# Part-ahead joins, closer search steps and alternating transpose banks in a retention plus two-layer expert kernel

## The chip, the cores and the metric

One core of a Trainium2 chip runs the whole program. The metric is the device time of one execution in microseconds (us); lower is better. Where a profile is shown, it is of one execution recorded by the hardware profiler.

## The reference, cut to what matters

Three blocks run one after the other on 3072 tokens of 512 features.

```python
# 1. retention (attention without softmax), 4 x 8 heads, 768 steps, 64 wide
state = gamma * state + k_t (outer) v_t ;  y_t = q_t @ state / 8
# 2. a dense layer: w_in 512 x 2048, w_out 2048 x 512
x2 = (s * relu(x @ w_in) ** 2 + b) @ w_out
# 3. eight experts, 512 -> 1024 -> 512, cap = 3072 / 8 = 384 tokens each
logits = x2 @ w_gate
for idx in argsort(-logits.flatten()):          # the highest (token, expert) pair first
    tok, e = idx // 8, idx % 8
    if assigned[tok] >= 0 or counts[e] >= cap: continue
    assigned[tok] = e; counts[e] += 1
for e in range(8):
    out[assigned == e] = relu(x2[assigned == e] @ w1[e]) @ w2[e]
```

The greedy assignment is done as up to eight searches: each finds by counting the threshold at which the next expert fills up, so the experts are known one after the other.

## The kernel before, in words

Every product of two float32 matrices is three matmuls on parts: a "high" part (`h`, `hh`, `gh`, `rh`), rounded by ScalarE, and a "low" part (`l`, `hl`, `gl`, `rl`), the rest, made by VectorE. The change touches the last 460 us: the end of block 2 and all of block 3.

- **The last dense blocks** (`x_last`, L672): 64 units of three 128x512 matmuls each; their four results are scaled by ScalarE (L675) and written to DRAM as `x2d` (L677).
- **A search** (`search`, with `begin` ahead of it). `begin` takes each token's best remaining expert, makes the one-hot `Eh`, and ScalarE copies it out as `EH` (L767), the stationary operand of the counts. Then come six steps; a step is a compare on VectorE (`cmp`, L772: 128x1512 against 63 thresholds in the first two, 128x744 against 31 in the other four), 24 small matmuls that count (L779), and a short VectorE chain (`sat`, `tr`, `jj`, `thr`) that ends in the next compare. A last count (`g`, 128x2), a sum over tokens (L865, `tots` L867) and two matmuls (L880, L881) give each token its place in the expert.
- **An index** (`index`): four one-hot comparisons (`big`, L915), 24 matmuls (L921), and `idx`, the token numbers of this expert. **A fetch** (`fetch`): three indirect DMAs of 128 rows of `x2d` each into `big` (GpSimd's queue, L935), 12 transposes (L945), `gh` and `gl`.
- **An expert** (`mlp`): for each of eight parts `f`, four `eh_unit`s (three 128x384 matmuls each, L997) make the hidden part, ScalarE makes `hh` (L1000), VectorE `hl` (L1006), and three `ey_unit`s (three 128x512 matmuls each, L1018) add it to the output. Weights come as `eraw` (512 KB a part, SyncE's queue, L966); `prep` splits them into `h` (ScalarE, L974) and `l` (VectorE, L975).

The order is set while the program is written out: `Weave` adds up planned costs of units on TensorE (490 for an `eh_unit`, 650 for an `ey_unit` or an `x_last` unit), and each side generator (searches, indexes, weights, fetches) goes on when that sum passes its due time. The numbers in the generators' `yield`s are therefore distances in planned TensorE nanoseconds. `Weave.until` lets the sides run on without units until an expert's `gh`, `gl` exist. Each engine executes its own instructions in the order written. PSUM has eight banks; the searches count into bank 6, the index uses 7, the experts' hidden parts 2 and 3, their outputs 0, 1 and 4, and the transposes 5 (for the first expert 4 and 5).

Of the kernel before, what the change touches and what calls it, by code (L numbers as in the profile page):

```python
# [20 lines left out]
F32 = mybir.dt.float32  # L21
F32R = mybir.dt.float32r
# [5 lines left out]
AF = mybir.ActivationFunctionType  # L28
OP = mybir.AluOpType
# [52 lines left out]
def kernel(  # L82
# [17 lines left out]
    PRO=1.5,  # L100
    PN=2,
    CY=(700, 1200, 650),
    SY=(5500, 5200, 4200, 3000, 2600, 1200),
    IY=(1500, 2700, 900),
    LG=(900, 880),
    FE=(7110, 3450),
    FZ=(8390, 160),
    BG=(800,),
    WARM=24,
):  # L110
    nc = tc.nc
# [6 lines left out]
    KC = Dm // 128  # L118
    NF = w64.shape[0]
    E, NF2 = w12.shape[0], w12.shape[1]  # L120
    CAP = N // E
    GT = CAP // 128
    NC = N // 128
# [12 lines left out]
    PE, ACT, DVE, POOL, SP = nc.tensor, nc.scalar, nc.vector, nc.gpsimd, nc.sync  # L136

    def bank(i):
        return psum.tile([128, 512], F32, name=f"b{i}", tag=f"b{i}")
# [69 lines left out]
    wb = bank(3)[:, 0:TB]  # L209
# [363 lines left out]
    while not a3.done:  # L573
        if conv.due < a3.due and PN not in READY:
            t = conv.due
# [5 lines left out]
    wv = Weave([conv])  # L581
# [16 lines left out]
    for blk in range(3, NB - 2):  # L598
        nxt = Side(attn(blk + 1, False) if blk < NB - 3 else attn2())
        wv.add(nxt)  # L600
        units = moe1((blk,), ((0, 1),), 2)
# [12 lines left out]
    ident = rt.tile([128, 128], F32, name="ident")  # L614
# [9 lines left out]
    ones_b = rt.tile([128, 128], BF, name="ones_b")  # L624
# [101 lines left out]
    def b3(ap, n):  # L726
        return ap[:, :, None].to_broadcast([128, NC, n])

    def b8(ap):
        return ap[:, None, :].to_broadcast([128, NC, E])  # L730
# [12 lines left out]
    def begin(i):  # L743


        Lm = rt.tile([128, NC, E], F32, name="Lm")
        if i:
            DVE.tensor_tensor(Lm, L, b8(pen), op=OP.add)
            src = Lm
        else:  # L750
            src = L
        m = rt.tile([128, NC], F32, name="m", bufs=2)
        mx = rt.tile([128, NC], F32, name="mx", bufs=2)
        DVE.tensor_reduce(m, src, axis=AX.X, op=OP.max)
        if i:
            yield BG[0]
        DVE.tensor_tensor(Lm, src, b3(m, E), op=OP.is_equal)
        DVE.tensor_tensor(Lm, Lm, b8(w8), op=OP.mult)
        DVE.tensor_reduce(mx, Lm, axis=AX.X, op=OP.max)
        if i:  # L760
            yield BG[0]
            DVE.tensor_tensor(mx, mx, Uf, op=OP.mult)
        Eh = rt.tile([128, NC, E], BF, name="Eh")
        DVE.tensor_tensor(Eh, b8(w8), b3(mx, E), op=OP.is_equal)

        EH = rt.tile([128, NC, 128 // E, E], BF, name="EH")
        ACT.activation(EH, Eh[:, :, None, :].to_broadcast([128, NC, 128 // E, E]), AF.Copy)  # L767
        ME[i] = (m, mx, EH.rearrange("p c r e -> p c (r e)"))

    def compare(m, thr, n):  # L770
# [5 lines left out]
    def count(EH, x, n):  # L776
        ps = bank(6)
        for c in range(NC):
            PE.matmul(ps[:, 0:n], EH[:, c, :], x[:, c, 0:n], start=(c == 0), stop=(c == NC - 1))  # L779
        return ps  # L780
# [10 lines left out]
    def search(i):  # L791
        last = i == E - 1
        m, mx, EH = ME.pop(i)
        if last:
            T = rt.tile([128, 1], F32, name="T")
            DVE.memset(T, NEG)
            yield SY[0]
        else:
# [3 lines left out]
            for s, w in enumerate(BW):  # L802
                n = (1 << w) - 1
                sh -= w
                yield SY[0] if s == 0 else SY[1] if n == NT else SY[2]
                cnt = count(EH, cmp, n)
# [39 lines left out]
        DVE.tensor_tensor(eq, eq, ug, op=OP.subtract)  # L846
        yield SY[3]

# [12 lines left out]
        DVE.tensor_tensor(rem, rem, ca[:, 0:1], op=OP.subtract)  # L861
        yield SY[4]

# [11 lines left out]
        DVE.tensor_tensor(rem, rem, s8, op=OP.add)  # L875
        yield SY[5]
        while i - 2 in SLOT or i - 2 >= 0 and i - 2 not in EREG:
# [13 lines left out]
    def index(i):  # L891

        while i not in SLOT:
            yield 200
        yield IY[0]
        s1 = SLOT.pop(i)
# [17 lines left out]
        for c in range(0, NC, 6):  # L914
            DVE.tensor_tensor(ob[:, c:c + 6, :], iota16[:, None, :].to_broadcast([128, 6, 128]),  # L915
                              lowp[:, c:c + 6, None].to_broadcast([128, 6, 128]), op=OP.is_equal)
            yield IY[2]
        for c in range(0, NC, 6):
            yield IY[2] if c else IY[1] - IY[2]
            for c in range(c, c + 6):  # L920
# [8 lines left out]
    def fetch(i):  # L929

        while i not in IDX or not X2DONE:
            yield 200
        xg = rt.tile([128, GT, Dm], F32, name="big", bufs=1)
        for t in range(GT):
            POOL.indirect_dma_start(out=xg[:, t, :], out_offset=None, in_=x2d[:, :],  # L935
                                    in_offset=bass.IndirectOffsetOnAxis(ap=IDX[i][:, t:t + 1], axis=0))
        yield FE[0] if i else FZ[0]
        while i - 2 >= 0 and i - 2 not in DONE or (i, 1) not in EW_ASKED:
            yield 200
        gh = ff.tile([128, KC, CAP], F32R, name="gh")  # L940
        gl = ff.tile([128, KC, CAP], F32R, name="gl")
        for kc in range(KC):
            pt = bank(5 if i or kc % 2 else 4)
            for t in range(GT):
                PE.transpose(pt[:, t * 128:(t + 1) * 128], xg[:, t, kc * 128:(kc + 1) * 128], ident)  # L945
            ACT.activation(gh[:, kc, :], pt[:, 0:CAP], AF.Identity, bias=cT[:, kc:kc + 1])
            DVE.scalar_tensor_tensor(gl[:, kc, :], pt[:, 0:CAP], cT[:, kc:kc + 1], gh[:, kc, :].bitcast(F32),  # L947
                                     op0=OP.add, op1=OP.subtract)
            if kc < 2:
                prep(i, kc)  # L950
            if kc < KC - 1:
                yield FE[1] if i else FZ[1]
        XG[i] = (gh, gl)

    DONE = set()
# [2 lines left out]
    EREG = {}  # L958

    EW_ASKED = set()  # L960

    def e_load(i, f):
        EW_ASKED.add((i, f))
        t = stage.tile([128, 2, 512], F32, name="eraw", tag="sa" if f % 2 else "sb")
        ERAW[i, f] = t
        SP.dma_start(t, w12[bass.ds(EREG[i], 1), f].rearrange("o p a n -> p (o a) n"))  # L966

    def e_split(i, f):
        raw = ERAW.pop((i, f))
        for a in range(2):  # L970
            n = 16 * (i % 2) + 2 * f + a
            hi = wpool.tile([128, 512], F32R, name=f"h{n}", tag=f"h{n}")
            lo = wpool.tile([128, 512], F32R, name=f"l{n}", tag=f"l{n}")
            ACT.activation(hi, raw[:, a, :], AF.Copy)  # L974
            DVE.tensor_tensor(lo, raw[:, a, :], hi.bitcast(F32), op=OP.subtract)  # L975
            EW[i, f, a] = (hi, lo)

    def prep(i, f):
        if f < NF2 and (i, f, 0) not in EW:
            e_split(i, f)  # L980
            if f + 4 < NF2:
                e_load(i, f + 4)
# [6 lines left out]
    def eh_unit(i, f, part):  # L989
        gh, gl = XG[i]  # L990
        wh, wl = EW[i, f, 0]
        if part == 0:
            PH[0] = bank(2 + f % 2)[:, 0:CAP]
        kc = part
        ks = slice(kc * 128, (kc + 1) * 128)
        for n, (a, b) in enumerate(((wh, gh), (wh, gl), (wl, gh))):
            PE.matmul(PH[0], a[:, ks], b[:, kc, :], start=(kc == 0 and n == 0), stop=(kc == KC - 1 and n == 2))  # L997
        if part == KC - 1:
            hh = ff.tile([128, CAP], F32R, name="hh")
            ACT.activation(hh, PH[0], AF.Relu)  # L1000
            HH[i, f] = [hh, PH[0]]

    def eh_out(i, f):
        hh, ph = HH[i, f]
        hl = ff.tile([128, CAP], F32R, name="hl")
        DVE.scalar_tensor_tensor(hl, ph, 0.0, hh.bitcast(F32), op0=OP.max, op1=OP.subtract)  # L1006
        HH[i, f] = (hh, hl)

# [21 lines left out]
    def mlp(i):  # L1030
        units = []

        for f in range(NF2 + 1):
            if f < NF2:
                for part in range(KC):
                    units.append((490, lambda f=f, part=part: eh_unit(i, f, part)))
            for t in range(GT):

                for g in (f - 1,) if f < NF2 - 1 else () if f < NF2 else (f - 2, f - 1):
                    if g >= 0:  # L1040
                        units.append((650, lambda g=g, t=t: ey_unit(i, g, t)))
                if f < NF2 and t == 0:
                    units.append((0, lambda f=f: (eh_out(i, f), prep(i, f + 2))))
                if f == NF2:
                    units.append((0, lambda t=t: e_out(i, t)))
        return units

    def searches():
        for i in range(E):
            yield from search(i)  # L1050
# [15 lines left out]
    def fetches():  # L1066
        for i in range(E):
            yield from fetch(i)

    list(begin(0))  # L1070
    wv = Weave([Side(searches()), Side(indexes()), Side(weights())])
    fill(len(order))
    X2DONE.append(1)
    p1.close()
    ff = ctx.enter_context(tc.tile_pool(name="ff", bufs=2))
    wv.add(Side(fetches()))
    for i in range(E):
        wv.until(lambda: i in XG)
        for u in mlp(i):
            wv.unit(*u)  # L1080
        DONE.add(i)
# [81 lines left out]
```

## Time and profile before

| | us |
|---|---|
| median of three runs | 1107.38 (1106.67 to 1112.36) |
| the profiled execution | 1106.38 |
| its span, first to last instruction | 1104.3 |
| TensorE busy / weight loads busy | 1006.6 (91%) / 877.4 (79%) |
| VectorE / ScalarE / GpSimd busy | 769.6 (70%) / 460.6 (42%) / 78.0 (7%) |

The times of the rows below are of the profiled execution, whose span leaves 2.1 us of its time outside. Busy times of matmuls overlap their successors, so a busy TensorE may still advance slowly. Mean TensorE clock over the span was 0.962 of full.

### The profile page before, as it was taken

The page shows a single profiled execution, that of the slowest core. Times are in us where ns is not written, and L with a number is a line of the kernel's source. Part 1 is how long each engine was busy: PE and PEld are TensorE (multiplying, and loading weights), DVE is VectorE, ACT ScalarE, POOL GpSimd, SP SyncE. Part 2 cuts the span into 40 slices and gives each one's busy share as a digit, 9 for nine tenths or more (in the row PEclk, how much of TensorE's full clock was granted, in tenths as well). Part 3 has the DMA queues.
Part 4 walks back from the last instruction along what each step waited for, and adds up shares of the span by engine and source line. Part 5 has one row for each costly group of instructions (what it writes and reads, how often), then busy time and mean ns, then how long its engine had stood idle before and what let it go on. Part 6 is the DMA issues. An engine that isn't in the chain of part 4 may idle for free.

```text
span 1104.3 us, 19566 instructions
## 1 busy us (share of the span) xinstructions
PE 1006.6 (91%) x7636; PEld 877.4 (79%) x7636; DVE 769.6 (70%) x1954; ACT 460.6 (42%) x978; POOL 78.0 (7%) x99
## 2 busy tenths in 40 slices
PE   5699999899999999999999998596888898888997
PEld 4698878889899989889988986484767777676786
DVE  2899992587887878787726243777868787876642
ACT  1367665344444444444436621233323333343442
POOL 3200010000000000000000000102020201111211
PEclk8899999899999999999999999598899999999999
DMA  8343433432121212121211002223242434333540
GB/s 305 109 143 115 153 135 124 135 105 56 60 68 48 68 49 77 50 66 49 68 39 33 1 1 99 84 96 97 76 133 98 134 97 144 114 106 106 173 142 29
DMA packets 35036, 104.48 MB, mean 95 GB/s; under 512 B 4736, under 2 KB 5248, under 8 KB 34944
## 3 DMA queue, kind: packets, MB, share of 16 engines
q1 hardware_dynamic: 30528, 89.60, 24.7%
q0 software_dynamic: 3840, 12.59, 3.4%
q8 instruction: 60, 0.98, 0.4%
q10 hardware_dynamic: 576, 1.05, 0.3%
q14 instruction: 32, 0.26, 0.1%
HBM read 90.64 MB, written 12.58 MB: 93 GB/s over the span
## 4 chain that ended last, share of the span: by engine, by line
PE 66%; DVE 15%; issue 8%; DMA 6%; ACT 3%; POOL 2%; SPq 0%; POOLq 0%; DVEq 0%; ACTq 0%
PE b L415 22%; PE b L444 18%; PE b L997 6%; PE b L1018 5%; PE b L672 3%; DMA big<-x2d,idx 3%; PE b L779 2%; DVE l L975 2%; PE b L348 2%; PE b L358 2%; PE b L328 2%; DVE cmp L772 2%; POOL big L935 2%; DVE raw L268 1%; DVE raw L253 1%
## 5 line engine op out<-in xcount | busy, mean ns | idle before, releaser
L467 DVE SCALAR_TENSOR_TENSOR scr<-tmp,wg 128x512 bf16<-128x512 f32 x288 | 198.0, 688 | 8.8 <-ACT tmp L454 4.0
L415 PE MATMUL b<-xh,h 128*128 128x256 f32 x704 | 200.0, 284 | 1.4 <-DVE xls L367 1.4
L415 PE MATMUL b<-xh,l 128*128 128x256 f32 x704 | 199.6, 284 | 0.0
L415 PE MATMUL b<-xl,h 128*128 128x256 f32 x704 | 199.6, 284 | 0.0
L418 ACT ACTIVATE r<-b 128x256 f32<-128x256 f32 x192 | 73.3, 382 | 208.0 <-PE b L415 199.9
L415 PEld LDWEIGHTS b<-xh,h 128*128 128x128 f32 x704 | 135.0, 192 | 10.2 <-DVE xls L367 1.6
L415 PEld LDWEIGHTS b<-xl,h 128*128 128x128 f32 x704 | 135.0, 192 | 5.5
L415 PEld LDWEIGHTS b<-xh,l 128*128 128x128 f32 x704 | 135.0, 192 | 0.0
L444 PE MATMUL b<-h,rl 128*128 128x512 f32 x320 | 126.0, 394 | 3.5 <-DVE rl L434 3.5
L444 PE MATMUL b<-h,rh 128*128 128x512 f32 x320 | 128.9, 403 | 0.0
L444 PE MATMUL b<-l,rh 128*128 128x512 f32 x320 | 126.0, 394 | 0.0
L434 DVE TENSOR_TENSOR rl<-r,rh 128x256 fp32r<-128x256 f32 x160 | 68.7, 430 | 46.7 <-ACT rh L427 46.2
L1018 PE MATMUL b<-h,hh 128*128 128x512 f32 x192 | 81.1, 423 | 13.3 <-ACT hh L1000 13.3
L997 PE MATMUL b<-gh,h 128*128 128x384 f32 x256 | 93.3, 364 | 0.0
L997 PE MATMUL b<-gl,h 128*128 128x384 f32 x256 | 88.0, 344 | 1.6 <-DVE gl L947 1.6
L1000 ACT ACTIVATE hh<-b 128x384 fp32r<-128x384 f32 x64 | 31.3, 489 | 137.8 <-PE b L997 136.3
L975 DVE TENSOR_TENSOR l<-eraw,h 128x512 fp32r<-128x512 f32 x128 | 82.3, 684 | 7.6 <-ACT h L974 7.6
L997 PE MATMUL b<-gh,l 128*128 128x384 f32 x256 | 87.5, 342 | 0.0
L1018 PE MATMUL b<-h,hl 128*128 128x512 f32 x192 | 79.0, 411 | 5.1 <-DVE hl L1006 4.6
L426 ACT ACTIVATE r<-r 128x256 f32<-128x256 f32 x192 | 79.9, 416 | 5.1
L1018 PE MATMUL b<-l,hh 128*128 128x512 f32 x192 | 77.3, 403 | 0.0
L444 PEld LDWEIGHTS b<-h,rl 128*128 128x128 f32 x320 | 60.1, 188 | 20.5 <-DVE rl L434 7.2
(191 smaller groups left out, 1816.9 us busy)
## 6 DMA issues: line engine op xcount, KB each, us to landing
eraw<-in_w_dram SPq DMA_DIRECT2D x64, 512.0 KB, 3.5
q<-in_qkv_dram SPq DMA_DIRECT2D x36, 512.0 KB, 4.8
raw<-in_w_dram SPq DMA_DIRECT2D x32, 512.0 KB, 4.3
first<-in_qkv_dram SPq DMA_DIRECT2D x24, 256.0 KB, 6.5
qdec<-in_dec_dram SPq DMA_DIRECT2D x24, 256.0 KB, 2.8
x2d<-tmp SPq DMA_DIRECT2D x20, 256.0 KB, 3.5
wg<-in_wgT_dram SPq DMA_DIRECT2D x4, 512.0 KB, 6.7
x2d<-tmp ACTq DMA_DIRECT2D x4, 256.0 KB, 2.0
```

The source lines that it names most:

```text
L328: PE.matmul(ps[s][:, p * 128:(p + 1) * 128], kT[ss, p, :], qT[ss, p, :], start=(p == 0), stop=True, skip_group_check=True)
L415: PE.matmul(ph, a[:, ks], b[:, kc, :], start=(n == 0), stop=(n == 3 * KC - 1))
L418: ACT.activation(r, ph, AF.Relu)
L426: ACT.activation(r, r, AF.Square)
L434: DVE.tensor_tensor(rl, r, rh.bitcast(F32), op=OP.subtract)
L444: PE.matmul(X2[blk][t], a[:, ts], b, start=(f == 0 and i == 0), stop=(f == NF - 1 and i == 2))
L467: DVE.scalar_tensor_tensor(scr, x, 1.0, WG[e], op0=OP.mult, op1=OP.mult, accum_out=of[:, e:e + 1])
L672: PE.matmul(XB[c], a[:, cs], b, start=(f == 0 and i == 0), stop=(f == NF - 1 and i == 2))
L975: DVE.tensor_tensor(lo, raw[:, a, :], hi.bitcast(F32), op=OP.subtract)
L997: PE.matmul(PH[0], a[:, ks], b[:, kc, :], start=(kc == 0 and n == 0), stop=(kc == KC - 1 and n == 2))
L1000: ACT.activation(hh, PH[0], AF.Relu)
L1018: PE.matmul(Y[i, t], a[:, ts], b, start=(f == 0 and j == 0), stop=(f == NF2 - 1 and j == 2))
```

## The change

- Numbers: the distances between a search's steps (`SY`), inside `begin` (`BG`) and inside an index (`IY`) get smaller; a fetch's distance from its DMAs to its first transpose (`FE[0]`) grows and that between its transposes (`FE[1]`) shrinks.
- `EH` is copied in four quarters instead of one instruction.
- Transposes alternate between banks 5 and 7; the first expert's use banks 4, 5, 0 and 1, and go by fetched tile instead of by feature block.
- An expert's outputs (`ey_unit`) follow its hidden parts by two instead of one, `prep` runs three parts ahead instead of two, and the low part of a weight is made at the next `prep`, not at once. `hh` and `hl` get a third buffer.
- After the last dense unit, 28 matmuls on constants (128x512, into bank 3, not read) stand in TensorE's order.

```diff
-    SY=(5500, 5200, 4200, 3000, 2600, 1200),
-    IY=(1500, 2700, 900),
+    SY=(3200, 3800, 3200, 2500, 2200, 800),
+    IY=(600, 1800, 800),
-    FE=(7110, 3450),
-    FZ=(8390, 160),
-    BG=(800,),
+    FE=(9000, 3000),
+    FZ=(8390, 1300),
+    BG=(450,),
...
-        ACT.activation(EH, Eh[:, :, None, :].to_broadcast([128, NC, 128 // E, E]), AF.Copy)
+        for c in range(0, NC, 6):
+            ACT.activation(EH[:, c:c + 6], Eh[:, c:c + 6, None, :].to_broadcast([128, 6, 128 // E, E]), AF.Copy)
+            if i:
+                yield BG[0]
...
-        while i - 2 >= 0 and i - 2 not in DONE or (i, 1) not in EW_ASKED:
+        while i - 2 >= 0 and i - 2 not in DONE or (i, 2) not in EW_ASKED:
...
+        if i == 0:
+            for f in range(3):
+                prep(i, f)
+            pts = [bank(b) for b in (4, 5, 0, 1)]
+            for t in range(GT):
+                for kc in range(KC):
+                    turn(pts[kc], t, kc)
+                if t < GT - 1:
+                    yield FZ[1]
+            prep(i, NF2)
...
-            pt = bank(5 if i or kc % 2 else 4)
+            if i:
+                pt = bank((5, 7)[kc % 2])
...
-            DVE.tensor_tensor(lo, raw[:, a, :], hi.bitcast(F32), op=OP.subtract)
+            ELOW.append((lo, raw[:, a, :], hi))
...
     def prep(i, f):
+        while ELOW:
+            lo, raw, hi = ELOW.pop(0)
+            DVE.tensor_tensor(lo, raw, hi.bitcast(F32), op=OP.subtract)
...
-                for g in (f - 1,) if f < NF2 - 1 else () if f < NF2 else (f - 2, f - 1):
+                for g in (f - 2,) if f < NF2 else (f - 2, f - 1):
...
-                    units.append((0, lambda f=f: (eh_out(i, f), prep(i, f + 2))))
+                    units.append((0, lambda f=f: (eh_out(i, f), prep(i, f + 3))))
...
+    wb = bank(3)
+    for _ in range(28):
+        wv.unit(220, lambda: PE.matmul(wb, ones_b, ones_b[:, None, :].to_broadcast([128, 4, 128]), start=True, stop=True))
```

What this does to the order is shown at three places. The first is VectorE, at the end of the first search. Before:

```order
L861 TENSOR_TENSOR rem<-rem,b_7542 128x1
L975 TENSOR_TENSOR l_7608<-eraw,h_7607 128x512
L975 TENSOR_TENSOR l_7612<-eraw,h_7611 128x512
L867 CAST tots<-b_7620 128x128
L869 TENSOR_TENSOR Uf<-Uf,ug 128x24
```

With the change:

```order
L864 TENSOR_TENSOR rem<-rem,b_7506 128x1
L870 CAST tots<-b_7576 128x128
...
L918 TENSOR_TENSOR big<-iota_6403,lowp 128x768
L762 TENSOR_TENSOR mx<-mx,Uf 128x24
L764 TENSOR_TENSOR Eh<-c_6397,mx 128x192
L918 TENSOR_TENSOR big<-iota_6403,lowp 128x768
L1004 TENSOR_TENSOR l_7569<-eraw,h_7568 128x512
L1004 TENSOR_TENSOR l_7572<-eraw,h_7571 128x512
```

The low parts of the first weights have moved from ahead of `tots` to behind the first two one-hot comparisons of the index.

The second place is ScalarE in the second or third expert, where the next search begins. Before:

```order
L1000 ACTIVATE hh<-b_9535 128x384
L974 ACTIVATE h_9566<-eraw 128x512
L974 ACTIVATE h_9570<-eraw 128x512
L767 ACTIVATE EH<-Eh 128x3072
L1000 ACTIVATE hh<-b_9595 128x384
```

With the change:

```order
L1026 ACTIVATE hh<-b_8801 128x384
L996 ACTIVATE h_8840<-eraw 128x512
L996 ACTIVATE h_8843<-eraw 128x512
L768 ACTIVATE EH<-Eh 128x768 x2
L1026 ACTIVATE hh<-b_8848 128x384
L768 ACTIVATE EH<-Eh 128x768
L996 ACTIVATE h_8906<-eraw 128x512
L996 ACTIVATE h_8909<-eraw 128x512
L768 ACTIVATE EH<-Eh 128x768
L1026 ACTIVATE hh<-b_8912 128x384
```

The one long copy, which stood between two `hh`, has become quarters with `hh` and weight splits between them.

The third place is TensorE at the end of the first expert (before) and, with the change, where the transposes for the second expert end. Before (of each count's 24 pairs the first is shown):

```order
L945 MATMUL b_8624<-ident,big 128x128 x3
L779 LDWEIGHTS EH
L779 MATMUL b_8630<-cmp,EH 128x31
...
L945 MATMUL b_8668<-ident,big 128x128 x3
L997 MATMUL b_8674<-gh,h_8518 128x384
L997 MATMUL b_8674<-gl,h_8518 128x384
L997 MATMUL b_8674<-gh,l_8519 128x384
```

With the change:

```order
L1044 MATMUL b_8233<-h_8387,hh 128x512
L1044 MATMUL b_8233<-l_8388,hh 128x512
L1044 MATMUL b_8233<-h_8387,hl 128x512
L947 MATMUL b_8745<-ident,big 128x128 x3
L1044 MATMUL b_8242<-h_8281,hh 128x512
L1044 MATMUL b_8242<-l_8282,hh 128x512
L1044 MATMUL b_8242<-h_8281,hl 128x512
L782 LDWEIGHTS EH
L782 MATMUL b_8758<-g_8721,EH 128x2
```

Before, the last transposes and counts stood between two experts with no expert unit among them; now the last transposes stand among the units of the expert that ends.

## Rows read from the trace of the kernel before

**Rows 1.** Windows: the join, then the eight experts; its first line names the columns

```profile
core 0: us, PE busy (x) PEld busy (x) DVE busy (x) ACT busy (x) POOL busy (x), PEclk, DMA share, GB/s
684.80:716.50 31.70, 12.86 (x122) 9.97 (x122) 21.09 (x62) 7.00 (x9) 3.68 (x3) 0.62 0.39 128
716.50:775.60 59.10, 48.39 (x426) 40.79 (x425) 43.62 (x132) 19.28 (x33) 6.36 (x9) 0.88 0.30 99
...
829.00:877.50 48.50, 42.28 (x372) 34.97 (x371) 39.24 (x114) 18.12 (x32) 6.75 (x9) 1.00 0.35 113
...
927.30:978.80 51.50, 44.65 (x378) 36.70 (x377) 39.98 (x119) 18.68 (x32) 6.57 (x9) 0.97 0.35 112
...
1026.90:1061.90 35.00, 34.58 (x198) 29.96 (x197) 20.55 (x35) 15.53 (x30) 3.43 (x5) 1.00 0.50 166
1061.90:1097.50 35.60, 35.60 (x177) 31.45 (x175) 11.99 (x20) 12.56 (x24) 4.64 (x9) 1.00 0.15 55
```

**Rows 2.** Waits of TensorE from 684.8 to 1097.5: total us, times, longest

```profile
PE b L779 <- DVE cmp L772: 14.5, 8, 3.0
PE b L1018 <- ACT hh L1000: 13.3, 5, 3.1
PE b L945 <- DMA big<-x2d,idx: 11.8, 16, 1.4
PE b L880 <- DVE tots L867: 6.1, 1, 6.1
```

**Rows 3.** Timeline of the join, TensorE: start, us, instruction, [idle before, releaser]

```profile
690.90 0.20 PE L880 MATMUL b<-stb,strict 128*128 128x48 bf16 x1 [6.12 <-DVE tots L867]
...
695.69 0.40 PE L672 MATMUL b<-h,l 128*128 128x512 f32 x1
...
713.56 1.12 PE L945 MATMUL b<-ident,big 128*128 128x128 f32 x4 [0.94 <-DMA big<-x2d,idx]
...
718.62 0.52 PE L997 MATMUL b<-gh,h 128*128 128x384 f32 x1
...
719.69 0.33 PE L997 MATMUL b<-gl,h 128*128 128x384 f32 x1
```

**Rows 4.** Timeline of the join, ScalarE and GpSimd

```profile
688.70 2.44 ACT L974 ACTIVATE h<-eraw 128x512 fp32r<-128x512 f32 x4 [6.07 <-DMA eraw<-in_w_dram]
...
701.11 0.33 ACTq L677 DMA_DIRECT2D x2d<-tmp  x1
706.69 1.14 POOL L935 DMA_INDIRECT big<-x2d,idx  x1 [123.28 <-DVE idx L926]
```

**Rows 5.** Timeline of VectorE in one search: durations and distances

```profile
855.77 0.28 DVE L810 SCALAR_TENSOR_TENSOR sat<-b,rem,ones_b 128x63 bf16<-128x63 f32 x1
857.39 1.73 DVE L772 TENSOR_TENSOR cmp<-m,thr 128x1512 bf16<-128x1512 f32 x1
...
859.45 0.55 DVE L1006 SCALAR_TENSOR_TENSOR hl<-b,hh 128x384 fp32r<-128x384 f32 x1
859.91 1.28 DVE L975 TENSOR_TENSOR l<-eraw,h 128x512 fp32r<-128x512 f32 x2
...
862.13 0.93 DVE L772 TENSOR_TENSOR cmp<-m,thr 128x744 bf16<-128x744 f32 x1
...
891.67 0.20 DVE L883 SCALAR_TENSOR_TENSOR s<-b,stb 128x48 f32<-128x48 f32 x1
...
894.39 0.36 DVE L764 TENSOR_TENSOR Eh<-c,mx 128x192 bf16<-128x192 f32 x1
...
896.31 0.18 DVE L898 SCALAR_TENSOR_TENSOR sl<-s 128x24 f32<-128x24 f32 x1
...
897.60 1.82 DVE L915 TENSOR_TENSOR big<-iota,lowp 128x768 f16<-128x768 f16 x2
```

**Rows 6.** Timeline of TensorE in one search: a count, and what follows it

```profile
873.23 0.77 PE L779 MATMUL b<-cmp,EH 128*128 128x31 bf16 x24
873.84 0.48 PE L1018 MATMUL b<-h,hh 128*128 128x512 f32 x1
```

More of the change, by code (lines that the diff above doesn't have):

```diff
@@ L941, in fetch, with turn @@
         gl = ff.tile([128, KC, CAP], F32R, name="gl")
-        for kc in range(KC):
-            pt = bank(5 if i or kc % 2 else 4)
-            for t in range(GT):
-                PE.transpose(pt[:, t * 128:(t + 1) * 128], xg[:, t, kc * 128:(kc + 1) * 128], ident)
+        def turn(pt, t, kc):
+            PE.transpose(pt[:, t * 128:(t + 1) * 128], xg[:, t, kc * 128:(kc + 1) * 128], ident)
+        if i == 0:
[8 more added lines that the diff above has]
+            prep(i, NF2)
+        for kc in range(KC):
+            if i:
+                pt = bank((5, 7)[kc % 2])
+                for t in range(GT):
+                    turn(pt, t, kc)
+            else:
+                pt = pts[kc]
             ACT.activation(gh[:, kc, :], pt[:, 0:CAP], AF.Identity, bias=cT[:, kc:kc + 1])
@@ L948, in fetch @@
                                      op0=OP.add, op1=OP.subtract)
-            if kc < 2:
+            if i and kc < 3:
                 prep(i, kc)
-            if kc < KC - 1:
-                yield FE[1] if i else FZ[1]
+            if i and kc < KC - 1:
+                yield FE[1]
         XG[i] = (gh, gl)
@@ L960 @@
     EW_ASKED = set()
+    ELOW = []
     def e_load(i, f):
@@ L998, in eh_unit @@
         if part == KC - 1:
-            hh = ff.tile([128, CAP], F32R, name="hh")
+            hh = ff.tile([128, CAP], F32R, name="hh", bufs=3)
             ACT.activation(hh, PH[0], AF.Relu)
@@ L1004, in eh_out @@
         hh, ph = HH[i, f]
-        hl = ff.tile([128, CAP], F32R, name="hl")
+        hl = ff.tile([128, CAP], F32R, name="hl", bufs=3)
         DVE.scalar_tensor_tensor(hl, ph, 0.0, hh.bitcast(F32), op0=OP.max, op1=OP.subtract)
```

## The prediction, made before the changed kernel ran

> **What bounds the kernel now.** I read the windows by expert first, then TensorE's waits, then the timelines of the join and of one search. The reader should see three regimes. In the last two experts TensorE hardly waits: 35.0 and 35.6 us an expert [rows 1]. In the experts ahead of them, beside which a search runs, an expert takes 48.5 to 59.1 us and VectorE is busy for 39 to 44 of them [rows 1]. The join between the dense layer and the first expert takes 31.7 us, at a granted clock of 0.62, in which TensorE is busy for 12.9 [rows 1]. So this stage is bound by TensorE at its end, and before by VectorE and TensorE waiting for each other in turn: 14.5 us for compares, 13.3 for `hh`, 11.8 for fetched rows and 6.1 for `tots` [rows 2].
>
> An expert with a search costs TensorE, without waits: 35.0 (one expert, with 12 transposes and 24 index matmuls at full clock [rows 1]), and the counts. A count holds TensorE for 0.61 us up to the next start, plus some 0.1 for the slower restart [rows 6]: 0.7. I take 0.85 where there are 63 columns. Four of 0.7, two of 0.85, the last count 0.7 and the three sums 0.4 make 5.6, together 40.6. The expert from 829.0 took 48.5, of which TensorE was idle for 48.5 - 42.3 = 6.2 [rows 1]; 48.5 - 40.6 - 6.2 = 1.7 us are in neither (restarts and clock). I keep these 1.7 for the sum.
>
> **The join.** In the old order the weights' low parts stand ahead of `tots`, and these wait for `h`, which waited 6.07 us for its DMA [rows 4]; so TensorE stood 6.12 us at L880 [rows 3]. In the new order `tots` comes first, and this wait goes. Closer steps put the last count of the first search 12 units of 0.69 us earlier among the dense units, less some 2.4 us, as the first count now comes before its compare and its `EH` are ready: 5.8 us earlier in all. The weights then land near 683 instead of 688.7 [rows 4].
>
> What is late next is the second search's first count, now inside the dense units: VectorE must first make four one-hots (0.9 each), two low parts (1.3) and a compare of 1.7 [rows 5], after the 3.7 us of index and `begin` arithmetic. I get 688.8 for the compare against 685.0 for TensorE, a wait of 3.8. The dense units end near 697, about as before (the last began at 695.69 [rows 3]), but with two counts and all index matmuls done. The last `x2d` write then leaves at 698 instead of 701.1 [rows 4], and the fetch starts when it has landed, near 701, instead of 706.7, when it had waited for `idx` [rows 4]. The third tile takes 713.56 - 706.69 = 6.9 us [rows 3, 4]: 708. On VectorE the four `gl` stand behind two low parts and the end of the last search step, so I let the first hidden part end at 714.3; before, at 720.0 (the last row of [rows 3]). Three counts that stood behind this point are done. The 28 constant matmuls (6.2 us by the pitch of 512 columns) run while the fetch is under way, so they are free; if the fetch were done at once they would cost 6. Bounds of the join: 9 us saved (no wait inside the dense units) to 3 lost (both waits of 4 to 6 us add up).
>
> On the clock there: I let the experts start at full clock. Before, their first nine matmuls took 0.52 us each and the later ones 0.33 [rows 3], some 0.15 each in pace, so this is worth 1.3 us.
>
> The Trainium skill ("TensorE: Matmul & The Clock Gate", Part 4: PE-mode transpose) says that transposes don't count as activity for the clock. By that rule the eight to twelve transposes behind the constant matmuls would not hold the clock, the 1.3 us would stay, and the sum below would be 1076. The trace agrees so far as the granted clock of the old join, with its transposes, is 0.62 [rows 1].
>
> **The experts with a search.** In the new order a search's last counts stand after 0.08, 0.98, 1.88, 2.77, 3.66 and 4.57 experts (counted by matmuls), so a search period is 0.9 expert instead of 1.0, and the last full search ends 0.6 of an expert earlier (4.57 instead of 5.19). No count moves out of the program; each period has the same work for fewer expert units. TensorE's floor of a period is 40.6 - 0.1 x 35.0 = 37.1. VectorE's is its 39.2 to 40.0 in such an expert [rows 1] less a tenth of an expert's own splits (16 `l` of 0.62, 8 `hl` of 0.5, 4 `gl` of 0.6: 16 us), so 38. They are nearly equal, and neither can be reached while they wait for each other.
>
> The waits removed: `EH` in quarters no longer holds `hh`, and outputs follow two parts later, so `hh` (13.3) goes, and `hl` with it; fetched rows (11.8) go, since a fetch now has 9000 planned ns instead of 7110, 1.9 us more, and each of these waits was 1.4 at most [rows 2].
>
> The waits that stay or grow are for compares. From L883 on, VectorE has one `hl` and two `l` (1.7), the chain from `s` to `Eh` (3.0), the index arithmetic (1.3), three one-hots (2.7), `hl` and two `l` again (1.7) and the compare (1.65) [rows 5]: 12.0 us. TensorE has 24 hidden-part matmuls at 0.175, nine output ones at 0.23 and two index pieces in between, 6.8 us. So it waits 5.2 us at the index and the first count. The second compare: one-hot 0.9, `hl` and `l` 1.7, `sat` to `thr` 1.6, compare 1.65, against 5.0 us on TensorE: wait 0.8. The later steps have 2.15 + 1.7 us on VectorE, 0.55 more with a `gl`, against 3.9 to 4.6 on TensorE with the count: no wait. Together 6.0.
>
> A period is then 37.1 + 6.0 + 1.7 = 44.8; I take 45. Before, the comparable figure was 48.5 to 51.5 for a whole expert, 45 to 48 without a tenth of one. Bounds: 41 (half of the compare waits, no rest) to 49 (every step also waits for VectorE).
>
> The Trainium skill ("Perfetto Trace Analysis", Identifying the Most-Contended Engine) holds weight loads, not busy matmuls, to be the measure of TensorE. Scaled by that, 34.97 us of loads against 31.45 in 35.6 [rows 1] would make its own work in the searched expert 39.6 instead of 40.6, a period 44 and the sum 1070.
>
> Alternating banks, third buffers and deeper `prep` cost no engine time; they are covered as long as weights are there. Loads are asked for three parts, some 13 us, ahead of need.
>
> **The sum.** First hidden part 714.3, last count of the second search 715; five periods of 45 to 940; 3.43 experts of 35.3 (the mean of the last two [rows 1]) are 121, and 4 for what the last search, of one count, still costs: 1065. From the last expert's end at 1097.5 [rows 1] to the span's end there were 6.8 us: 1072. Outside the span 2.1: 1074. The profiled execution lay 1.0 under the median of the runs: **1075 us**.
>
> **Rivals.**
> - *VectorE becomes the pace.* For it: 39 of 48.5 us busy already [rows 1], and low parts, `hl` and `gl` stand between the steps of a search in one queue. Against: the steps as walked through fit. At 49 a period, 5 x 4 more: 1095.
> - *The periods don't get shorter.* If the wait for compares simply takes all that `hh` and the fetch give back, searches of 50 a period leave the join and the expert without a search: 1101. Against: the order shows the searches closer.
> - *Better than walked.* If TensorE finds the one-hots and compares in time (VectorE ahead by the third `hh` buffer), 41 a period: 1055.
> - *Slower: weights late.* A part's `eraw` buffer is now released one part (4.3 us) later, as its low part is made at the next `prep`; the load into it starts later, and `h` stands in ScalarE's queue ahead of the next `hh`. It decides from the point where a load takes over some 13 us. In the old join ScalarE waited 6.07 us for a load asked for just before [rows 4]. Each us by which the 64 parts are late is 64: 1139.
>
> **How the numbers follow.** Forecast 0.60, better 0.10, VectorE's pace 0.19, periods unchanged 0.07, late weights 0.04. The likeliest alone lies in 1064 to 1086 (period 43 to 47). The range for 8 in 10 leaves out the late weights and the ends of the others: 1056 to 1097. This kernel can be told from no change from about 0.5% (5.5 us) on: faster than 1101.8 are the forecast, better, pace and half of the unchanged, 0.92; slower 0.04, same 0.04.
>
> **What would show it.** Right: no wait at the sum over tokens in the join; `x2d`'s last write near 698 and the fetch near 701; no wait of output matmuls for `hh`; counts waiting for compares mostly at the first of a search, 3 to 5 us, six times; searched stretches of 45 per 0.9 expert; the last three experts near 35. Wrong: VectorE over 95% busy over the first four experts with waits at all counts (its pace); ScalarE waiting for `eraw` (late weights); the granted clock below 0.9 in the searched experts, which the sum doesn't contain.

## The result, and the profile after

The changed kernel took 1077.12 us (median of four runs, 1075.79 to 1079.82), the kernel before 1107.20 us beside it (1106.67 to 1112.36): a ratio of 0.972, 95% interval 0.9688 to 0.9751. The profiled execution took 1078.43 us, its span 1076.7 us. Repeated later, beside three of the variants, the same changed kernel took 1068.08 us; the experiments come back to that, and measure against the repeat.

Windows of the changed kernel, cut at the join, at the last count `g` of each search, and in the last two experts (columns as in [rows 1]):

```profile
684.80:712.70 27.90, 21.56 (x232) 15.20 (x232) 21.54 (x61) 8.64 (x16) 3.04 (x3) 0.88 0.43 138
712.70:719.60 6.90, 5.36 (x16) 4.65 (x16) 3.77 (x14) 1.86 (x4) 0.00 (x0) 0.50 0.01 2
719.60:760.60 41.00, 38.31 (x358) 32.82 (x357) 35.61 (x111) 15.30 (x29) 3.87 (x5) 1.00 0.29 97
760.60:805.10 44.50, 39.95 (x358) 34.35 (x357) 39.16 (x115) 17.86 (x34) 6.02 (x9) 0.92 0.39 126
...
893.60:941.30 47.70, 42.11 (x364) 35.55 (x363) 38.10 (x115) 18.38 (x34) 7.33 (x8) 0.93 0.34 109
...
1000.00:1035.00 35.00, 35.00 (x183) 31.74 (x182) 16.09 (x28) 16.03 (x31) 5.38 (x10) 1.00 0.51 166
```

The searched periods took 41.0, 44.5, 44.9, 43.6 and 47.7 us, 221.7 in all (forecast 5 x 45); the last experts run at 35.0, as before. TensorE's waits from 684.8 to 1090 (total us, times, longest) answer to [rows 2]:

```profile
PE b L782 <- DVE cmp L775: 14.7, 8, 3.5
PE b L1023 <- DVE hl L1032: 6.9, 3, 3.6
PE b L924 <- DVE big L918: 3.7, 7, 1.8
PE b L1023 <- issue: 2.5, 1, 2.5
PE b L1044 <- ACT hh L1026: 2.2, 1, 2.2
```

The wait for `tots` in the join (6.1) and the sixteen for fetched rows (11.8) are gone, and that of output matmuls for `hh` fell from 13.3 to 2.2. The wait for compares is as large as before. New is one that the forecast did not have: hidden-part matmuls (L1023) that wait for an `hl`, since `hl` still reads the PSUM bank that they write into (banks 2 and 3 take turns from part to part). The timeline of the join on TensorE answers to [rows 3]:

```profile
689.59 1.44 PE L782 MATMUL b<-cmp,EH 128*128 128x63 bf16 x24 [3.47 <-DVE cmp L775]
...
698.86 0.40 PE L672 MATMUL b<-h,l 128*128 128x512 f32 x1
...
704.64 1.89 PE L1106 MATMUL b<-ones_b 128*128 128x512 bf16 x8
708.17 0.76 PE L782 MATMUL b<-cmp,EH 128*128 128x31 bf16 x24 [1.65 <-DVE cmp L775]
...
711.58 1.09 PE L947 MATMUL b<-ident,big 128*128 128x128 f32 x4
...
714.93 0.69 PE L1023 MATMUL b<-gl,h 128*128 128x384 f32 x1 [1.54 <-DVE gl L968]
...
719.26 0.52 PE L1023 MATMUL b<-gh,l 128*128 128x384 f32 x1
```

and that of ScalarE to [rows 4] (the first of GpSimd's fetches started at 703.41):

```profile
681.63 1.15 ACT L996 ACTIVATE h<-eraw 128x512 fp32r<-128x512 f32 x2 [7.15 <-DMA eraw<-in_w_dram]
...
700.01 0.33 ACTq L677 DMA_DIRECT2D x2d<-tmp  x1
```

The join has the forecast shape some 2 us late: a wait of 3.47 us for a compare inside the dense units (forecast 3.8), the last `x2d` write at 700.0 (698), the fetch at 703.4 (701). Its last stretch is worse: all 15 hidden-part matmuls up to 719.6 ran at the lower of the clock's two levels (0.50 granted, 13 of them 0.52 us each, where 0.33 is usual later on), and the second search's last count came at 719.6 instead of 715.

### The profile page after: what moved, and what is told of

It is laid out like the page before. It is cut to its first block, busy times and chain, and to the rows that moved or that the text cites. A ratio compares the mean times of both kernels' runs of the same rounds, so it can differ in the third digit from the quotient of the medians.

```text
span 1076.7 us, 19597 instructions
## 1 busy us (share of the span) xinstructions
PE 1003.4 (93%) x7664; PEld 879.8 (82%) x7664; DVE 769.2 (71%) x1954; ACT 462.7 (43%) x1002; POOL 77.0 (7%) x99
## 4 chain that ended last, share of the span: by engine, by line
PE 65%; DVE 21%; issue 8%; DMA 2%; ACT 1%; POOL 1%; another core or an unknown queue 0%; SPq 0%; POOLq 0%; DVEq 0%; ACTq 0%
PE b L415 23%; PE b L444 18%; PE b L1023 6%; PE b L1044 4%; PE b L672 3%; DVE l L1004 3%; PE b L782 2%; PE b L348 2%; DVE big L918 2%; PE b L358 2%; DVE cmp L775 2%; PE b L328 2%; DVE hl L1032 1%; DVE raw L268 1%; DMA first<-in_qkv_dram 1%
## 5 line engine op out<-in xcount | busy, mean ns | idle before, releaser
L1023 PE MATMUL b<-gh,h 128*128 128x384 f32 x256 | 94.3, 368 | 9.4 <-DVE hl L1032 6.9
L1023 PE MATMUL b<-gl,h 128*128 128x384 f32 x256 | 89.5, 349 | 1.5 <-DVE gl L968 1.5
L1023 PE MATMUL b<-gh,l 128*128 128x384 f32 x256 | 89.7, 351 | 0.0
L996 ACT ACTIVATE h<-eraw 128x512 fp32r<-128x512 f32 x128 | 72.7, 622 | 10.2 <-DMA eraw<-in_w_dram 9.8
L1044 PE MATMUL b<-h,hl 128*128 128x512 f32 x192 | 76.1, 396 | 0.4 <-DVE hl L1032 0.4
```

The costliest lines, as they stand in the source:

```text
L1044: PE.matmul(Y[i, t], a[:, ts], b, start=(f == 0 and j == 0), stop=(f == NF2 - 1 and j == 2))
```

## The experiments

After the first measurement came three series, each with the kernel before beside it; a ratio is to the kernel before of the same series. The first series held old distances, new distances only, outputs one part behind and index later; the second held low parts at once, `EH` in one, one bank and no constants; the third held both repeats and the last two rows. "Join" is the start of the second `gh,h` matmul of the first expert, "experts" the time from there to the last `h,hl` matmul, both in us from TensorE's timeline of the profiled execution, which can lie some us off the median (1077.89 us for "low parts at once", 3.5 above it).

| kernel | median us | ratio, 95% interval | join | experts |
|---|---|---|---|---|
| before (its first trace) | 1107.20 | 1 | 717.7 | 379.5 |
| with the change, first | 1077.12 | 0.972 (0.9688 to 0.9751) | 715.7 | 353.9 |
| with the change, repeated | 1068.08 | 0.9653 (0.9631 to 0.9675) | 714.0 | 345.3 |
| old distances | 1074.23 | 0.9691 (0.9669 to 0.9713) | 714.3 | 353.7 |
| old distances, repeated | 1075.59 | 0.9712 (0.9687 to 0.9737) | 712.9 | 353.9 |
| new distances only | 1093.33 | 0.9867 (0.985 to 0.9883) | 723.4 | 362.3 |
| outputs one part behind | 1081.95 | 0.9773 (0.9754 to 0.9793) | 716.6 | 356.7 |
| low parts at once | 1074.43 | 0.971 (0.969 to 0.9729) | 723.8 | 344.9 |
| `EH` in one | 1071.05 | 0.9675 (0.9652 to 0.9698) | 716.9 | 347.4 |
| transposes in one bank | 1070.05 | 0.9674 (0.9655 to 0.9693) | 714.7 | 345.4 |
| no constant matmuls | 1066.87 | 0.9637 (0.9615 to 0.9658) | 714.3 | 345.6 |
| index later | 1071.12 | 0.9671 (0.9652 to 0.969) | 715.4 | 347.1 |
| later, no constants | 1071.66 | 0.9685 (0.9665 to 0.9706) | 713.7 | 348.3 |
| later, wider | 1066.45 | 0.9639 (0.9619 to 0.9659) | 711.4 | 344.3 |

The kernel before kept its time over the series (1106.19 to 1107.22 us) and the old distances theirs (1074.23 and 1075.59), but the changed kernel moved by 9 us. So a variant measured once, in another series than the repeat, differs surely only where it differs by more than that; for the others the traces have to speak. What the variants of the first two series were expected to take was counted from 1077.12 us, so those ranges lie some 9 us high.

Theory: the shorter search periods give the gain in the experts, the new order of low parts that in the join. Rival: the edits around them (outputs two parts behind, buffers, `EH` in quarters, banks, late low parts) do it, whatever the distances.

### Distances and the rest apart

The old distances of searches, indexes and `begin`, with all other edits; and the new ones alone, in the kernel before:

```diff
-    SY=(3200, 3800, 3200, 2500, 2200, 800),
-    IY=(600, 1800, 800),
-    BG=(450,),
+    SY=(5500, 5200, 4200, 3000, 2600, 1200),
+    IY=(1500, 2700, 900),
+    BG=(800,),
```

> The changed kernel with the old distances (SY, IY, BG, FE as before), all else as changed. Theory S (the structure gives the gain: outputs two parts behind, EH in quarters, low parts later, two banks take the waits for hh, fetched rows and tots away): it stays within 8 us of the changed kernel's 1077, losing some 5 us in the join, where idx is late again; no output matmul waits over 1 us for hh. Rival D (the closer steps give it, since searches then never run out of expert units): the counts without units between experts are back, 4 to 5 us each for five experts, and it takes 1095 to 1105.

> The kernel before with the new distances in searches, begin and index alone (SY, IY, BG). Theory S: hh still waits behind the long EH copy (13 us) and transposes for fetched rows (12 us), and only the join gains; 1092 to 1104. Rival D: a period of 0.9 expert at 45 us gives most of the gain, 1080 to 1088.

Old distances: 1074.23 us. Beside the first result that read as if the closer steps gave nothing, but the repeat below showed that this comparison was off. New distances alone: 1093.33 us, inside the range of theory S, but not with the waits it names. TensorE's waits from 700 on in it:

```profile
PE b L779 <- ACT EH L767: 11.4, 3, 4.6
PE b L1018 <- DVE hl L1006: 8.3, 4, 3.6
PE b L945 <- DMA big<-x2d,idx: 5.3, 4, 2.7
PE b L779 <- DVE cmp L772: 5.1, 4, 2.0
...
PE b L1018 <- ACT hh L1000: 3.1, 1, 3.1
```

Waits for `hh` fell from 13.3 to 3.1 us and those for fetched rows from 11.8 to 5.3, where theory S had them stay. The experts got 17 us shorter, but counts now come to `EH` before it is copied (11.4 us in three places), and the join got longer: it kept its wait of 5.18 us for `tots`, and the first expert began 5.8 us later than before.

### The changed kernel once more, beside the old distances

No edit; and the same edit as above.

> The kernel with the change itself once more, beside the others of this call. Its trace held two places where several engines stood for 2 to 3 us without a visible reason (914.4 to 918.1 on VectorE and 918.1 to 920.9 on TensorE; 964.5 to 968.0 on VectorE behind an hh that ScalarE began 1.5 us late); no trace of the other variants has such a place. Theory A, that these pauses belong to that one recorded execution and its session: here no such waits, and 1069 to 1073 us. Rival B, that they belong to this order of instructions: the same pauses at the same instructions, and 1075 to 1079 us again.

> The kernel with the change and the old distances of the searches and indexes once more (1074.23 us the first time), now beside the kernel with the change on one chip. Theory A, that the closer steps give nothing on top of the changed structure: within 3 us of the kernel with the change, or faster than it. Rival B, that they are worth something there too, and were hidden by the pauses in the kernel with the change: 4 to 8 us slower than it.

1068.08 us (1066.12 to 1070.20, five runs) and 1075.59 us: the expectation of 1069 to 1073 was right in kind, if 1 us high, and in this series the distances are worth 7.5 us in the new structure after all (the intervals of the ratios do not touch). The profiled execution of the first measurement had pauses that are not in this one. The timelines of the changed kernel, first measurement, at two places, the second count of the last full search and the part behind the last search:

```profile
915.37 0.93 PE L782 MATMUL b<-cmp,EH 128*128 128x63 bf16 x24
...
918.12 0.28 DVE L813 SCALAR_TENSOR_TENSOR sat<-b,rem,ones_b 128x63 bf16<-128x63 f32 x1 [3.58 <-remote]
...
920.93 0.46 PE L1023 MATMUL b<-gh,h 128*128 128x384 f32 x1 [2.46 <-issue]
...
961.60 0.23 PE L868 MATMUL b<-ones_b,stb 128*128 128x128 bf16 x1
...
967.48 0.49 ACT L1026 ACTIVATE hh<-b 128x384 fp32r<-128x384 f32 x1 [5.09 <-PE b L1023]
...
968.62 0.44 PE L1023 MATMUL b<-gh,h 128*128 128x384 f32 x1 [2.38 <-DVE hl L1032]
```

and the same instructions in the repeat:

```profile
912.35 0.93 PE L782 MATMUL b<-cmp,EH 128*128 128x63 bf16 x24
...
913.32 0.28 DVE L813 SCALAR_TENSOR_TENSOR sat<-b,rem,ones_b 128x63 bf16<-128x63 f32 x1 [2.28 <-PE b L782]
...
916.18 0.44 PE L1023 MATMUL b<-gh,h 128*128 128x384 f32 x1 [0.74 <-DVE hl L1032]
...
955.48 0.23 PE L868 MATMUL b<-ones_b,stb 128*128 128x128 bf16 x1
...
958.12 0.49 ACT L1026 ACTIVATE hh<-b 128x384 fp32r<-128x384 f32 x1 [1.85 <-PE b L1023]
```

VectorE's `sat` began 2.75 us after the start of its count on TensorE (915.37), in the repeat 0.97 (912.35): 1.8 us late. ScalarE's `hh` began 5.88 us after the sum over tokens (961.60), in the repeat 2.64 (955.48): 3.2 us late. The `hl` behind each came late, and TensorE waited for its bank (the first wait is put down to "issue", but ends as that `hl` does): 1.7 and 2.4 us more than in the repeat, where the second of these waits isn't there. Each wait was followed by matmuls at half pace (seven and ten at 0.52 to 0.53 us). Against the repeat the period with the first pause was 3.1 us longer (47.7 to 44.6), the tail from the last full search's last count to the last output matmul 4.3 (128.4 to 124.1); the join and the other periods make up 3.0 of the 10.4 us between the spans. Why VectorE and ScalarE stood there, and whether they did in the other three executions of the first measurement, which have no trace, stays open. But those were as slow (1075.79 to 1079.82 us, all above the repeat's highest, 1070.20), so what made them slow was in each of the four, and pauses of one trace are only a candidate for it.

The repeat's windows by period, and TensorE's waits from 684.8 on, here and with the old distances:

```profile
717.60:758.60 41.00, 38.31 (x358) 32.82 (x357) 35.85 (x111) 15.32 (x29) 3.87 (x5) 1.00 0.31 97
758.60:802.95 44.35, 39.98 (x358) 34.27 (x358) 39.07 (x116) 17.84 (x34) 5.52 (x9) 0.92 0.39 126
802.95:847.70 44.75, 40.77 (x362) 35.17 (x362) 39.69 (x121) 18.70 (x35) 6.27 (x9) 0.92 0.40 135
847.70:890.60 42.90, 38.07 (x356) 32.44 (x356) 38.65 (x114) 18.09 (x34) 7.30 (x9) 1.00 0.38 126
890.60:935.20 44.60, 40.76 (x362) 34.36 (x362) 38.00 (x115) 18.35 (x34) 6.92 (x8) 0.96 0.36 117
```

```profile
PE b L782 <- DVE cmp L775: 12.8, 8, 3.5
PE b L1023 <- DVE hl L1032: 5.2, 3, 3.6
PE b L924 <- DVE big L918: 3.7, 7, 1.8
PE b L1044 <- ACT hh L1026: 2.2, 1, 2.2
PE b L1023 <- DVE gl L968: 2.0, 1, 2.0
```

```profile
PE b L782 <- DVE cmp L775: 19.7, 14, 3.4
PE b L1023 <- DVE gl L968: 7.7, 6, 3.4
```

The time is as rival B of the repeated old distances has it, 4 to 8 us slower. But neither `hh` nor fetched rows are waited for there either (0.4 us in one place), as theory S of the first of these experiments had it, so the closer steps aren't needed for that; alone they remove the larger part of these waits too, as the run before showed. What they add to the rest is that six counts no longer wait for a compare, and five hidden parts no longer for `gl`; waits for `hl`, one-hots and `hh` grow in return. From 684.8 to the last output matmul TensorE stood idle for 28.4 us (374.8 less 346.42 busy) against 32.8 (382.3 less 349.46): 4.5 of the 7.5 us. The rest is busy time, at a mean granted clock of 0.97 against 0.95.

### Outputs two parts behind, and EH in quarters

```diff
-                for g in (f - 2,) if f < NF2 else (f - 2, f - 1):
+                for g in (f - 1,) if f < NF2 - 1 else () if f < NF2 else (f - 2, f - 1):
```

> The changed kernel with outputs one part behind the hidden parts as before. If the second part of distance is what removes the waits for hh and hl: output matmuls wait for hl or hh 2 to 4 us a search, 1087 to 1100. Rival (EH in quarters alone is enough): within 3 us of the changed kernel, 1074 to 1080.

```diff
-            ACT.activation(EH[:, c:c + 6], Eh[:, c:c + 6, None, :].to_broadcast([128, 6, 128 // E, E]), AF.Copy)
+            if c == 0:
+                ACT.activation(EH, Eh[:, :, None, :].to_broadcast([128, NC, 128 // E, E]), AF.Copy)
```

> The kernel with the change, with EH copied in one instruction of some 2.8 us instead of four quarters (the distances stay). Theory A, that the quarters are what removed the waits for hh: these come back, about 2 to 3 us a search in five searches, 1087 to 1092 us. Rival B, that the outputs two parts behind cover a late hh anyway: TensorE's waits for hh stay under 4 us, 1076 to 1080 us.

One part behind: 1081.95 us, 14 more than the repeat, though of another series. It lies below the range of 1087 to 1100. TensorE's waits with outputs one behind, from 684.8 on:

```profile
PE b L782 <- DVE cmp L775: 9.4, 6, 3.5
PE b L1044 <- DVE hl L1032: 6.2, 6, 3.6
...
PE b L1044 <- ACT hh L1026: 6.0, 2, 3.3
```

Output matmuls wait 12.2 us for `hh` and `hl` (2.6 in the repeat: 2.2 and 0.4). In return hidden parts no longer wait for the bank that `hl` reads (5.2 in the repeat). Of the 14.0 us between the two profiled executions, 6.2 are idle time of TensorE from 684.8 to the last output matmul (34.6 against 28.4 us) and the rest is busy time, at a mean granted clock of 0.95 against 0.97. The second part of distance is the largest of the terms that were taken out one at a time. `EH` in one piece: 1071.05 us, whose interval overlaps the repeat's; the waits for `hh` are 3.4 us in one place. So the quarters were not what freed `hh`, and the rival in that expectation was right.

Not taken out alone were the fetch's distances (`FE`, `FZ`), the third buffers and the deeper `prep`. Waits for fetched rows stay under 3 us in every variant that keeps the new `FE`, so that larger distance is the likeliest to have removed them; that is argued, not shown.

### Low parts at the next prep, and the constant matmuls

```diff
-            ELOW.append((lo, raw[:, a, :], hi))
+            DVE.tensor_tensor(lo, raw[:, a, :], hi.bitcast(F32), op=OP.subtract)
```

> The kernel with the change, with the low part of a weight made at once, behind its high part, as before the change. Theory A, the prediction's: in the join VectorE again takes the low parts, which wait for the weights, ahead of the sum over tokens; TensorE's wait there of about 6 us comes back, part of it hidden; the experts are unchanged: 1081 to 1086 us. Rival B, that the deferral matters in the experts, since a low part that waits for ScalarE's h stands ahead of compares on VectorE: more waits for compares in every search too, 1087 to 1097 us. Rival C, no effect: 1075 to 1079 us.

1074.43 us, 6.4 more than the repeat. The join of this kernel on TensorE:

```profile
686.75 0.20 PE L883 MATMUL b<-stb,strict 128*128 128x48 bf16 x1 [5.17 <-DVE tots L870]
...
699.37 0.92 PE L782 MATMUL b<-cmp,EH 128*128 128x63 bf16 x24 [4.16 <-DVE cmp L775]
```

The wait for `tots` is back, and the join is 9.8 us later in this profiled execution, which is itself 3.5 us above the median; the experts take 344.9 us against 345.3: the deferral works in the join alone, as forecast.

```diff
-        wv.unit(220, lambda: PE.matmul(wb, ones_b, ones_b[:, None, :].to_broadcast([128, 4, 128]), start=True, stop=True))
+        wv.unit(220, lambda: None)
```

> The kernel with the change, without the 28 matmuls on constants (their place in the planned order is kept, so nothing else moves). Theory A, that they neither cost nor give anything: in the trace with the change they ended at about 706.5 while the fetched rows came at 708.2, and the first hidden-part matmuls ran at half pace all the same; then 1075 to 1079 us, and a first hidden part that starts at 712 to 713.5 and runs at 0.52 us a matmul. Rival B, that they keep the clock from falling further: the counts, the transposes and the first hidden parts run longer at the low clock, first-part end later by 2 us or more, 1079 to 1083 us. Rival C, that they stand in the way: 1071 to 1075 us.

1066.87 us, not told apart from the repeat. Windows of 3 us in the join (the column after the busy times is the granted clock), with the constant matmuls (the repeat) and then without:

```profile
708.00:711.00 3.00, 1.89 (x32) 1.48 (x32) 2.86 (x10) 0.54 (x2) 0.00 (x0) 1.00 0.15 61
...
714.00:717.00 3.00, 3.00 (x11) 2.98 (x10) 1.02 (x2) 0.00 (x0) 0.00 (x0) 0.50 0.02 5
```

```profile
705.00:708.00 3.00, 1.04 (x25) 0.96 (x25) 2.26 (x9) 0.00 (x0) 2.27 (x3) 0.50 0.50 126
708.00:711.00 3.00, 2.69 (x33) 2.23 (x33) 1.92 (x5) 0.00 (x0) 0.00 (x0) 0.50 0.42 137
711.00:714.00 3.00, 1.27 (x6) 0.78 (x6) 2.73 (x14) 2.00 (x4) 0.00 (x0) 0.95 0.00 0
714.00:717.00 3.00, 3.00 (x12) 2.92 (x13) 1.34 (x3) 0.00 (x1) 0.00 (x0) 0.62 0.00 0
```

With the constants the granted clock is 1.00 through counts and transposes (every window from 696 to 714); without them it falls to 0.50 there, behind counts with waits of 2.0 us between them, and is back at 0.95 from 711 to 714. A low stretch at the first hidden parts follows in both, nine or ten matmuls at 0.52 to 0.53 us behind waits for `gl` of 1.5 to 2.0 us. So the constants take away the first low stretch and not the second, and the second search's last count comes at the same time (717.59 and 717.72).

### One bank, and other distances

```diff
-                pt = bank((5, 7)[kc % 2])
+                pt = bank(5)
```

> The kernel with the change, with the transposes of the later experts all in bank 5 (TensorE's order unchanged, only the buffer differs). Theory A, that with 3000 planned ns between two groups of transposes the bank is free again in time: 1075 to 1080 us, waits of transposes for gl under 3 us in all. Rival B, that a gl that stands behind compares and one-hots on VectorE holds the bank: waits for gl of 1 to 2 us in several of the 21 places, 1083 to 1092 us.

1070.05 us, an interval that overlaps the repeat's, and no transpose that waits for `gl`: theory A in the waits, and the second bank is worth nothing that can be seen here.

The first distance of an index at 2600 instead of 600 (`IY`); this without the constant matmuls; and that with wider first steps of a search:

```diff
-    SY=(3200, 3800, 3200, 2500, 2200, 800),
-    IY=(600, 1800, 800),
+    SY=(4200, 4400, 3200, 2500, 2200, 800),
+    IY=(2600, 1800, 800),
```

> The changed kernel with an index that begins 2000 planned ns later (IY 2600 instead of 600), so that the next search's EH and first compare come ahead of the one-hots on VectorE. If the first compare waits because the one-hots stand ahead of it: waits of counts for compares fall from 14.7 to under 7 us and the time to 1067 to 1072. Rival: the one-hots only move the wait to the second compare, hl or the fetch (idx is 2 us later in the join too): 1075 to 1082.

> The kernel with the change, with the first distance of an index at 2600 instead of 600 and without the matmuls on constants: the two edits that were fastest alone. If their gains add up (6 and 10 us against the first runs of the kernel with the change) 1061 us; if each only escaped the pauses of that kernel, 1066 to 1071 us, like each alone.

> As the previous, with the first two distances of a search at 4200 and 4400 instead of 3200 and 3800. Theory A, that the waits for compares at the first two counts of a search (8 of 10.3 us with the index later) go when TensorE comes to them later: waits for compares under 5 us, 1062 to 1067 us. Rival B, that the time goes elsewhere, as a search takes a longer part of an expert: 1068 to 1074 us.

1071.12, 1071.66 and 1066.45 us. What looked like a gain of 6 us for the later index, beside the first result, is a loss of 3 beside the repeat, or nothing, as the intervals touch; it adds up with nothing. With it alone, the waits for compares are 10.3 us, not under 7. The wider steps gain 5.2 us on the same kernel without them, of the same series (1071.66; the intervals don't touch), 4.0 of it in the experts (348.3 to 344.3) and 2.3 in the join. The time is in theory A's range but its reason is not: waits for compares are 12.2 us (14.3 without the wider steps, 12.8 in the repeat), where under 5 had been expected. No variant beats the changed kernel by more than can be told.

## Why the prediction was right, and where not

- **The sum.** Forecast 1075, measured 1077.12 and, repeated, 1068.08. By its own steps for the repeat: last count of the second search 717.6 (forecast 715), five periods 217.6 (225), from there to the last output matmul 124.1 (125), to the end of the span 7.0 (6.8), outside it 1.8 (2.1), and no 1.0 between this execution and the median. The first result lies 2 us from the forecast partly by luck, as errors met: by the same steps its join was 4.6 us late (719.6) and its last stretch 3.4 too long (128.4), against 3.3 less in the periods (221.7) and 2.3 because the profiled execution lay 1.3 above the median instead of 1.0 below.
- **The period.** The mean was 43.5 us (44.3 in the first measurement) against 45. The split was wrong. In the repeat's five periods (717.6 to 935.2) TensorE waited 8.2 us for compares and 2.8 for one-hots, where 30 were forecast for the two, most of it at counts with 63 columns, the first two of a search, as walked through; beside them came 5.6 for `hl` (3.6 in one place) and 2.2 for `hh`. With 0.8 of small ones that is 19.6, or 3.9 a period instead of 6.0. The rest of a period went the other way: TensorE was busy for 39.6 (197.90 us in the five), where the sum had 37.1 + 1.7; the granted clock was 0.92 to 0.96 in three of the five. The term that was mis-sized is the 5.2 us a search at the index and the first count, which measured 1.9 (6.5 us at three first counts and 2.8 at one-hots in the five); the term that was missing is the bank that an `hl` behind one-hots and a compare holds. The Trainium skill ("Perfetto Trace Analysis", Identifying the Most-Contended Engine), which measures TensorE by its weight loads (and by the share of peak work done) rather than by busy matmuls, led to a period of 44 in the prediction, nearer to the 43.5. That is by two errors that meet: it put TensorE's own part of a period at 37.8, where 39.6 were measured, beside waits of 6.0, where it was 3.9. Loads were busy for 34.27 of 44.35 us in a period, so no run here shows them as the limit.
- **What removed the waits.** "`EH` in quarters no longer holds `hh`, and outputs follow two parts later" was right in its second half alone: 14 us (11.4 of them in the experts) against 3 that can't be told from none. Fetched rows are no longer waited for, as forecast, but which edit did it was not tested alone. "Closer steps" and the rest each shorten the experts without the other: by 17.2 us (379.5 to 362.3) and 25.6 (to 353.9). Together it is 34.2 and not 42.8, which fits that both remove most of the waits for `hh` and fetched rows.
- **The join.** "This wait goes" holds, and is shown by the low parts made at once. The first search's last count came 5.1 us earlier (679.65 before, 674.56 in the repeat; forecast 5.8), but the first expert got nothing of the closer steps: alone they made the join 5.8 us later, and with the rest it is no earlier than with the old distances (714.0 against 714.3 and 712.9). What they do there is to bring the second search's last count ahead, to 717.6 instead of 733.8 and 732.5.
- **The clock.** Experts that start at full clock, 1.3 us, did not come. The Trainium skill ("TensorE: Matmul & The Clock Gate", Part 4: PE-mode transpose) says that transposes don't count as activity for the clock. The trace doesn't decide whether that is the reason. In the repeat the transposes ran at 1.00, behind constant matmuls and counts, and the low stretch (0.50 from 714 to 717) came behind them, but behind a wait of 1.96 us for `gl` as well. Without the constants the transposes ran at 0.50 (708 to 711), yet the clock was back at 0.95 behind them before it fell again.
- **The rivals.** VectorE as the pace: its busy share in a period was 85 to 90% (38.00 of 44.60 to 38.65 of 42.90), and not every step waited. Late weights: in the repeat ScalarE waited for `eraw` 0.8 us in all from 684.8 on; the one long wait (7.15 us before 681.63 in the first measurement) is that for the first expert's weights, as before [rows 4]. Unchanged periods: with the old distances, five periods took 231.8 us (last counts at 732.52 and 964.33), 46.4 each, against 251.3 before (735.24 to 986.58), 50.3 each; with the change it is 43.5.

## What to carry to other kernels

When two engines wait for each other in turn, giving the consumer one more step of distance (outputs two parts behind, with a third buffer) can be worth more than moving the producer closer; edits that remove the same wait don't add up, so measure each with and without the other. Ask of each matmul who still reads the bank that it writes into, not only who makes its operands. Before reading small differences between variants, run the reference of the comparison again beside them: here it moved by 9 us, and the verdicts on the distances and on the later index with it.

## What was not expected of the hardware

- The same program took 1077.12 us (four runs) and 1068.08 us (five runs) in two measurements, while the kernel before took 1107.20 and 1107.22 beside them; the trace of the first shows two places where an engine began 1.8 and 3.2 us late for no reason that it shows, that of the second none.
- After waits of 2.46 and 2.38 us TensorE ran at half pace for seven to ten matmuls: the period and the tail lost 3.1 and 4.3 us, of which the waits make up 1.7 and 2.4.
- The number of matmuls at half clock at the start of the first expert was 15 in the first execution and about ten in the repeat, of one program.
